# Causal attention with memory and a gated MLP: pairing the mask matmuls, one addition on VectorE, the feature's exponential to SBUF, updates out of the turning step

## The chip, the cores and the metric

The kernel runs on one core of a Trainium2 chip, as one program. The metric is the device time of an execution in microseconds (us). The core's engines work side by side, each through its own queue in order: TensorE (PE; its weight loads are PEld), VectorE (DVE), ScalarE (ACT), GpSimd (POOL) and SyncE (SP), which issues the transfers (DMA). SBUF is the working memory, PSUM the memory that matmuls write.

## The reference, cut to what matters

```python
def _layernorm(x, axis=-1, eps=1e-5): (x - mean) / sqrt(var + eps)

def _A_ref(x, wq, wk, wv, wo, beta):          # attention with memory, S=2048, D=640
    H = 32; Dh = D // H; N = 4; L = S // N    # Dh = 20, L = 512
    q, k, v = x @ wq, x @ wk, x @ wv          # each as (B, H, N, L, Dh)
    phi = lambda t: where(t > 0, t + 1.0, exp(t))
    M = 0; z = 0
    for s in range(N):
        logits = einsum("bhqd,bhkd->bhqk", qs, ks) * Dh ** -0.5 + mask   # causal, -1e9
        a_dot = softmax(logits) @ vs
        a_mem = (phi(qs) @ M) / (phi(qs) . z + 1e-6)
        o = g * a_mem + (1.0 - g) * a_dot     # g = sigmoid(beta), per head
        M = M + phi(ks)^T @ vs;  z = z + sum_l phi(ks)
    return o @ wo

def _B_ref(x, w_in, w_sp, b_sp, w_out):       # gated MLP, F = 1728, Fh = 864
    z = gelu(x @ w_in);  z1 = z[..., :Fh];  z2 = layernorm(z[..., Fh:])
    g = w_sp @ z2 + b_sp                      # mixes the 2048 rows
    return (z1 * g) @ w_out

x = x + _A_ref(layernorm(x));  x = x + _B_ref(layernorm(x))   # twice, same weights
```

## The kernel before

Every float32 operand of a large matmul is split into a high and a low float16 part, and a product is three matmuls (high by high, high by low, low by high). Each of the two layers has three stages: attention (class `Attention`, L594), the MLP's input half with the last four row tiles of attention's output (`phase1b`, L302), and the spatial half (`phase2`, L400). The change touches attention alone.

**The loop of attention.** `run` (L1034) goes through 64 pairs of heads (4 segments of 512 rows, 16 pairs each). Five steps `t` deal with two pairs; `STEPS` (L533) says what a step takes. In a step, in this order:

- `combine` (L1002) finishes an earlier pair: VectorE scales `pv` (PSUM) into `ab` (SBUF, four row tiles by two heads by 41 columns, of which `a` is the product with v's high part and the row sum, `b` that with v's low part), then GpSimd adds: in the first segment `o = a + b` (L1018); in later ones, where `o` already holds the memory's part, `a = a + o` (L1017) and then L1018.
- `by_queries` (L936) makes logits with queries on the partitions (`mp`, one PSUM buffer), and VectorE takes the maxima of the rows (L959; L956 for two heads' tiles at once) into `mxs`.
- `by_keys` (L905) makes them with keys on the partitions (`es`, one PSUM buffer), and ScalarE takes the exponential into P (L933). Only the causal part is made: key tile j has 512 - 128 j columns of queries. `POFF` (L530) is where a tile lies in P's 1280 columns, `KCH` and `QCH` say which tiles share a step.
- `maxes` (L973), in the turning step (every fifth, t % 5 = 2): the maxima are turned by TensorE (`mtp`, in the one small PSUM buffer "ms"), split into two parts `mr` by ScalarE and VectorE (L981), and written by DMA into rows of the queries, so that `es` comes out with the maximum subtracted.
- work that was posted for this step: `out` (below) and its like.
- `pvs` (L986): TensorE multiplies P's high and low parts PH and PL by v. `cast` (L962) makes PH on ScalarE and PL on GpSimd (in two halves of 640 columns).
- `until` spreads dense projections over the steps: `value` (v, `vps`), `unit` (q and k, `qps`, `kps`) and `project` (output, `yps`). They share two PSUM buffers "dn", so a third has to wait until one of them is read out. `read` (L806, `num`) reads the memory and `update` (L839, `mup`) adds to it, both in the buffer "ms".

**The mask.** After the logits of a step, `emit` (L889) adds -60000 x 60000 or 0 to each diagonal tile by two matmuls for each of two heads (`mask`, L880): a step matrix as weights, a 64-column identity `g.eye` as what moves, 64 columns each. Where a step has two tiles, it has two diagonal tiles, so eight such matmuls.

**The features.** `out` (L763) reads a finished q or k projection: its high part (ScalarE, L770), relu (L773), low part (VectorE, L774). In the same step, later in the program, `features` (L782) takes the exponential in place in PSUM (L783) and VectorE makes min(exp, 1) + relu (L786 for q, L788 for k). Segment 0 needs no q features, segment 3 no k features: 30 of each in the two layers. For k, `keys` (L791) splits the result again (L793, L794), a DMA turns it into `pk` (one buffer), and `update` is posted at least three steps later in a step whose t % 5 is in `UPD` (L537) and which is not that of a read or the one behind it.

**What sets the order.** TensorE's order is the program's own (`manual_schedule`, L1199). On the other engines a scheduler orders the instructions by a model of their times, with the restriction that later work of a step stays behind its maximum or exponential (`behind`).

## Time and profile before

| | |
|---|---|
| median of 3 runs | 2308.2 us (2304.68 to 2310.23) |
| the profiled execution | 2313.21 us, its span 2311.5 us |
| granted TensorE clock, mean | 0.986 |
| first attention | about 75 to 600 us |
| second attention | about 1190 to 1735 us |
| TensorE, busy slices of 40 | 5 to 9 tenths, mostly 8 and 9 |

A profile is of one execution. The span runs from the first to the last instruction on the core, and the device time lies 1.7 us over it. In a group's row stand line, engine, operation, what it writes and reads, its shape, its count, then the busy time, the mean of one in ns, and the idle time before it with who ended it. "Who waited" rows give us and times. TensorE's matmuls are pipelined: the busy time counts the whole of each, though the next begins before it ends.

### The profile page before, as it was taken

What the parts mean: (1) busy time and instruction counts of PE and PEld (TensorE: products, weight loads), DVE (VectorE), ACT (ScalarE), POOL (GpSimd) and SP (SyncE); (2) the same over time, 40 slices, a digit from 0 to 9 for tenths busy, and PEclk for the clock granted to TensorE, in tenths of its full rate; (3) what the DMA queues carried; (4) which work ended last, traced back from release to release, by engine and by line L of the source; (5) the groups of instructions that cost most, each with busy time, mean ns of one, the idle gap of its engine ahead of it and who ended that gap; (6) DMA issues with size and microseconds to landing.
All of it is one profiled execution on the core that took longest, in us unless ns stands there. A gap on an engine that the chain in (4) does not pass through costs nothing.

```text
span 2311.5 us, 52604 instructions
## 1 busy us (share of the span) xinstructions
PE 2167.8 (94%) x21706; PEld 1306.2 (57%) x21706; DVE 1372.8 (59%) x2577; ACT 1139.0 (49%) x1344; POOL 987.0 (43%) x976
## 2 busy tenths in 40 slices
PE   5888889999899999999998989999989999999998
PEld 3455555666555555555554556566665555555554
DVE  7678878777754544343327786777756443534331
ACT  3578788888532322121126987888863322212110
POOL 2387889999610000000104988899991100000000
PEclk9999999999899999999999999999999999999999
DMA  5566665345743687566634465443565347756561
GB/s 167 148 159 157 169 165 133 84 119 133 212 127 86 150 231 158 160 156 162 148 86 107 113 149 144 124 102 106 139 172 127 94 118 201 164 155 163 154 147 47
DMA packets 512113, 325.60 MB, mean 141 GB/s; under 512 B 411488, under 2 KB 454368, under 8 KB 507520
## 3 DMA queue, kind: packets, MB, share of 16 engines
q1 hardware_dynamic: 511872, 322.23, 54.5%
q8 instruction: 170, 2.79, 0.5%
q14 instruction: 71, 0.58, 0.1%
HBM read 148.46 MB, written 85.61 MB: 101 GB/s over the span
## 4 chain that ended last, share of the span: by engine, by line
PE 56%; DMA 4%; POOL 4%; DVE 3%; ACT 3%; issue 2%; SPq 1%; DVEq 0%; ACTq 0%; POOLq 0%
PE gp L450 23%; PE zp L363 13%; PE cyp L479 8%; POOL PL L970 3%; PE qps L756 2%; PE pv L998 2%; PE vps L697 2%; PE kps L756 1%; PE mp L895 1%; DMA th<-xnhl 1%; PE yps L729 1%; PE yp L340 1%; ACT P L933 1%; PE es L895 1%; DVE mxs L959 1%
## 5 line engine op out<-in xcount | busy, mean ns | idle before, releaser
L970 POOL TENSOR_TENSOR PL<-P,PH 128x640 f16<-128x640 f32 x380 | 535.5, 1434 | 53.3 <-PE pv L998 43.6
L450 PE MATMUL gp<-zh,wt 128*128 128x432 f16 x2048 | 462.3, 346 | 0.0
L450 PEld LDWEIGHTS <-wt 128*128 128x128 f16 x3072 | 300.5, 98 | 257.6
L959 DVE TENSOR_REDUCE mxs<-mp 128x2 f32<-128x1024 f32 (+2 forms) x384 | 320.0, 861 | 140.5 <-PE mp L886 139.0
L933 ACT ACTIVATE P<-es,sc 128x1024 f32<-128x1024 f32 (+1 forms) x256 | 271.5, 1060 | 99.1 <-PE es L886 84.9
L465 POOL MEMSET un<- 128x64 f16 x32 | 5.0, 155 | 665.9 <-DMA ut<-un 632.7
L363 PEld LDWEIGHTS <-th 128*128 128x128 f16 x1920 | 188.6, 99 | 173.5 <-DMA th<-xnhl 9.7
L450 PE MATMUL gp<-zl,wt 128*128 128x432 f16 x1024 | 270.6, 346 | 0.0
L453 ACT ACTIVATE u<-gp,bsp,un 128x864 f32<-128x864 f32 x32 | 34.2, 1070 | 431.1 <-PE gp L450 419.6
L968 ACT CAST PH<-P 128x1280 f16<-128x1280 f32 x192 | 239.7, 1248 | 1.6
L272 POOL TENSOR_TENSOR lnrs<-lnve,mhalf 128x1 f32<-128x1 f32 x96 | 60.2, 635 | 421.2 <-DVE lnve L271 374.5
L427 DVE TENSOR_REDUCE am<-wr 128x1 f32<-128x2048 f32 x32 | 73.1, 2286 | 210.2 <-DMA wr<-in_B_w_sp_dram 210.2
L970 POOL TENSOR_TENSOR PL<-Pb,PH 128x640 f16<-128x640 f32 x124 | 177.1, 1454 | 12.4 <-PE pv L998 8.0
L697 PE MATMUL vps<-wvh,xt 128*128 128x320 f16 x640 | 156.6, 313 | 25.5 <-DVE relu L788 19.6
L479 PE MATMUL cyp<-wuh,ut 128*128 128x320 f16 (+1 forms) x896 | 165.1, 301 | 5.8 <-DMA ut<-un 5.8
L895 PEld LDWEIGHTS <-qk 64*128 64x128 f16 (+1 forms) x2048 | 78.2, 94 | 160.4 <-issue 140.0
L479 PEld LDWEIGHTS <-ut 128*128 128x128 f16 (+1 forms) x1344 | 132.1, 98 | 61.6 <-DMA ut<-un 6.6
L998 PE MATMUL pv<-vs,PL 128*128 128x41 f16 x2560 | 157.0, 181 | 4.7 <-POOL PL L970 4.3
L998 PE MATMUL pv<-vs,PH 128*128 128x41 f16 x2560 | 159.5, 182 | 1.1 <-DVE ab L1014 0.8
L363 PE MATMUL zp<-wi1h,th 128*128 128x432 f16 x640 | 151.2, 352 | 7.8 <-DMA th<-xnhl 7.6
L895 PE MATMUL es<-qk 64*128 64x512 f16 (+3 forms) x1024 | 124.8, 300 | 27.7 <-ACT P L933 20.1
L363 PE MATMUL zp<-wi0h,th 128*128 128x432 f16 x640 | 148.3, 346 | 0.0
(189 smaller groups left out, 4294.5 us busy)
## 6 DMA issues: line engine op xcount, KB each, us to landing
wr<-in_B_w_sp_dram SPq DMA_DIRECT2D x32, 1024.0 KB
qk<-st SPq DMA_DIRECT2D x256, 120.0 KB
z<-z SPq DMA_DIRECT2D x32, 432.0 KB
cz<-z SPq DMA_DIRECT2D x32, 432.0 KB
xt<-in_A_x_dram SPq DMA_DIRECT2D x32, 320.0 KB
st<-qhl SPq DMA_DIRECT2D x40, 256.0 KB
st<-khl SPq DMA_DIRECT2D x40, 256.0 KB
x<-x SPq DMA_DIRECT2D x32, 320.0 KB
```

Of the source, the lines that this page charges most:

```text
L363: nc.tensor.matmul(zp[:, n, :FHH], a[:, k, :], b[:, k, c:c + FHH], start=(k == 0 and j == 0), stop=(k == KD - 1 and j == 2))
L427: nc.vector.tensor_reduce(am, wr, AX.X, ALU.max, apply_absolute_value=True)
L450: nc.tensor.matmul(gp[:, n, :FHH], wt[:, k // 8, a, k % 8, :], b[:, k, n * FHH:(n + 1) * FHH], start=(k == 0 and j == 0), stop=(k == NT - ...
L479: nc.tensor.matmul(yp[:, n, :320], a[:kn[k], k, :], b[:kn[k], k, n * 320:(n + 1) * 320], start=(k == 0 and j == 0), stop=(k == KO - 1 and ...
L697: nc.tensor.matmul(ps, a[:, k, c], b[:, k, n * 320:(n + 1) * 320], start=(i == 0), stop=(i == 14))
L756: nc.tensor.matmul(ps, a[:, k, c], b[:, k, :], start=(i == 0), stop=(i == 14))
L895: nc.tensor.matmul(out[:, h, o:o + w], a[r, ac], b[r, bc], start=o == 0, stop=False, skip_group_check=True)
L933: g.exp = nc.scalar.activation(P, E, AF.Exp, scale=g.esc)
L959: e = nc.vector.tensor_reduce(mx[:, :, n, j], mp[:, :, o:o + w], AX.X, ALU.max)
L968: nc.scalar.copy(PH, P[:, h])
L970: (nc.gpsimd if h == 0 or n < self.N - self.TAIL else nc.vector).tensor_tensor(PL[:, c], P[:, h, c], PH[:, c], ALU.subtract)
L998: nc.tensor.matmul(pv[:, i, h, :], x[:, c:c + 128], v[:, j, h0 + h, :], start=(j == 0 and x is PH), stop=(j == i and x is PL), skip_group_ ...
```

## The change

Four edits:

- **Mask.** Where a step has two tiles, one matmul adds the mask to both diagonal tiles: the identity is there twice (128 columns) and the output is a view of two pieces of 64 columns. For that the second key step takes tiles 3 and 1 in this order, and P's columns change places (`POFF`).
- **Additions.** The first addition of `combine` goes from GpSimd to VectorE, and is now `a + b`; the one with the memory's part stays on GpSimd. In the first segment none is left on GpSimd.
- **Features.** The exponential is taken right behind relu, and into a tile `fe` in SBUF (one buffer) rather than in place in PSUM.
- **Updates.** `pk` gets a second buffer, and `UPD` loses the 2, the turning step.

```diff
--- before.py
+++ after.py
@@ -527,14 +527,14 @@
 NU = 5
 UH = [range(6 * m, 6 * m + 6) if m < 4 else range(24, 32) for m in range(NU)]
 TH = [range(min(128 * m // DH, UH[m][0]), (128 * m + 127) // DH + 1) for m in range(NU)]
-POFF = [0, 512, 1024, 896]
-KCH = ((0,), (1, 3), (2,))
+POFF = [0, 640, 1024, 512]
+KCH = ((0,), (3, 1), (2,))
 QCH = ((3,), (2, 0), (1,))
 STEPS = ((0, 0, 0), (0, 1, 0), (0, 2, 1), (1, 0, 0), (1, 1, 0))
 BIG = 60000.0
 PVS = ((0, 5, 0), (0, 6, 1), (1, 8, 0), (1, 8, 1))
 CAST = ((0, 2, 0), (0, 3, 1), (1, 4, 0), (1, 5, 1))
-UPD = (2, 3, 4, 0)
+UPD = (3, 4, 0)
 RD = (-6, -1, 9, 14, 24)
 
 
@@ -543,16 +543,17 @@
 
 
 
-    g.eye = cp.tile([128, 64], F16, name="eye")
+    g.eye = cp.tile([128, 128], F16, name="eye")
     g.step = {nm: cp.tile([128, 192], F16, name="step" + nm) for nm in "qk"}
     with tc.tile_pool(name="tmp", bufs=1) as tp, tc.tile_pool(name="acp", bufs=1, space=PSUM) as pp:
         f = tp.tile([128, 192], F32, name="fmask")
-        for t, n, b, sg, op in ((g.eye, 64, 0, 1, ALU.not_equal), (g.step["q"], 192, -64, 1, ALU.is_ge), (g.step["k"], 192, 64, -1, ALU.is_ge)):
+        for t, n, b, sg, op in ((g.eye[:, :64], 64, 0, 1, ALU.not_equal), (g.step["q"], 192, -64, 1, ALU.is_ge), (g.step["k"], 192, 64, -1, ALU.is_ge)):
             nc.vector.memset(f, 0.0)
             for h in range(2):
                 v = f[64 * h:64 * h + 64, :n]
                 nc.gpsimd.affine_select(v, v, [[sg, n]], op, BIG if op is ALU.not_equal else -BIG, base=b, channel_multiplier=-sg)
             nc.vector.tensor_copy(t, f[:, :n])
+        nc.vector.tensor_copy(g.eye[:, 64:], g.eye[:, :64])
 
         g.gate = cp.tile([128, H], F32, name="gate")
         g.iomg = cp.tile([128, H], F32, name="iomg")
@@ -771,31 +772,31 @@
             if feature:
                 r = self.u2.tile([128, L], F32, tag="tmp", name="relu")
                 nc.scalar.activation(r, ps, AF.Relu, scale=g.rq if q else g.rk)
+                e = self.u1.tile([128, L], F32, tag="fe", name="fe")
+                nc.scalar.activation(e, ps, AF.Exp, scale=g.rq if q else g.rk)
             nc.vector.scalar_tensor_tensor(hl[:, 1], ps, QS, hl[:, 0], ALU.mult, ALU.subtract)
             self.stack(nm, s, m, hl)
             if feature:
                 if self.now is None:
-                    features(r)
+                    features(r, e)
                 else:
-                    self.half.setdefault(self.now, []).append(lambda: features(r))
-
-        def features(r):
-            nc.scalar.activation(ps, ps, AF.Exp, scale=g.rq if q else g.rk)
+                    self.half.setdefault(self.now, []).append(lambda: features(r, e))
+
+        def features(r, e):
             if q:
                 self.phq[m] = self.u4.tile([128, L], F32, tag="phq", name="phq")
-                nc.vector.scalar_tensor_tensor(self.phq[m], ps, 1.0, r, ALU.min, ALU.add)
+                nc.vector.scalar_tensor_tensor(self.phq[m], e, 1.0, r, ALU.min, ALU.add)
             else:
-                nc.vector.scalar_tensor_tensor(r, ps, 1.0, r, ALU.min, ALU.add)
+                nc.vector.scalar_tensor_tensor(r, e, 1.0, r, ALU.min, ALU.add)
                 self.post(3 if self.now is not None and self.now < -5 else 1, lambda: keys(r))
 
         def keys(ph):
             hl = self.u2.tile([128, 2, L], F16, tag="hl", name="phl")
             nc.scalar.mul(hl[:, 0], ph, g.sig)
             nc.vector.scalar_tensor_tensor(hl[:, 1], ph, g.sig, hl[:, 0], ALU.mult, ALU.subtract)
-            self.pk_of = s, m
-            self.pk = self.u1.tile([128, 2, 4, 128], F16, tag="pk", name="pk")
-            nc.sync.dma_start(self.pk.rearrange("p i t c -> p (i t) c"), hl.rearrange("p i c -> p (i c)"), transpose=True)
-            work = lambda: self.update(s, m)
+            pk = self.u2.tile([128, 2, 4, 128], F16, tag="pk", name="pk")
+            nc.sync.dma_start(pk.rearrange("p i t c -> p (i t) c"), hl.rearrange("p i c -> p (i c)"), transpose=True)
+            work = lambda: self.update(s, m, pk)
             if self.now is None:
                 self.half.setdefault(-8, []).append(work)
             else:
@@ -836,11 +837,10 @@
 
         self.post(1, out)
 
-    def update(self, s, m):
+    def update(self, s, m, pk):
 
         g, nc = self.g, self.nc
-        assert self.pk_of == (s, m), (self.pk_of, s, m)
-        pkh, pkl = self.pk[:, 0], self.pk[:, 1]
+        pkh, pkl = pk[:, 0], pk[:, 1]
         n = len(TH[m])
         hs = slice(TH[m][0], TH[m][0] + n)
         v = self.vs[s % 2]
@@ -881,10 +881,15 @@
 
         g, nc = self.g, self.nc
         r = slice(64 * h, 64 * h + 64)
-
-        c = o + 64 * s
-        nc.tensor.matmul(out[:, c:c + 64], g.step[nm][r, 64 - 64 * s:192 - 64 * s], g.eye[r], start=False, stop=s == 1,
-                         skip_group_check=True)
+        n = len(o)
+        if n == 1:
+            v = out[:, h, o[0] + 64 * s:o[0] + 64 * s + 64]
+        else:
+            d = o[1] - o[0]
+            b = o[0] - o[0] % d
+            v = out[:, h, b:b + 2 * d].rearrange("p (n r c) -> p n r c", n=2, c=64)[:, :, (o[0] - b) // 64 + s, :]
+        e = g.eye[r, :64] if n == 1 else g.eye[r].rearrange("p (n c) -> p n c", n=2)
+        nc.tensor.matmul(v, g.step[nm][r, 64 - 64 * s:192 - 64 * s], e, start=False, stop=s == 1, skip_group_check=True)
 
     def emit(self, todo):
 
@@ -893,10 +898,10 @@
             for h in range(2):
                 r = slice(64 * h, 64 * h + nr)
                 nc.tensor.matmul(out[:, h, o:o + w], a[r, ac], b[r, bc], start=o == 0, stop=False, skip_group_check=True)
+        out, nm, o = todo[0][0], todo[0][8], [e[9] for e in todo]
         for half in range(2):
-            for out, _, _, _, _, _, _, _, nm, o in todo:
-                for h in range(2):
-                    self.mask(out[:, h], nm, h, o, half)
+            for h in range(2):
+                self.mask(out, nm, h, o, half)
 
     def pair(self, n):
 
@@ -1013,9 +1018,9 @@
         ab = self.pl2.tile([128, 4, 2, 41], F32, tag="ab", name="ab")
         nc.vector.tensor_tensor(ab, T, rs.unsqueeze(3).to_broadcast((128, 4, 2, 41)), ALU.mult)
         a, b = ab[:, :, :, 0:DH], ab[:, :, :, DH + 1:]
+        nc.vector.tensor_tensor(a if s > 0 else o, a, b, ALU.add)
         if s > 0:
-            nc.gpsimd.tensor_tensor(a, a, o, ALU.add)
-        nc.gpsimd.tensor_tensor(o, a, b, ALU.add)
+            nc.gpsimd.tensor_tensor(o, a, o, ALU.add)
         if h0 + 2 < UH[m][-1] + 1:
             return
 
```

**ScalarE, a k projection of the first segment.** `khl`, `relu` and `kps` (now `fe`) are the projection's high part, relu and exponential, `phl` the high part of the feature, P the exponentials of the logits, PH their high part, `mr` the turned maxima. Before:

```order
L770 ACTIVATE khl<-kps 128x512
L773 ACTIVATE relu<-kps,sc 128x512
L933 ACTIVATE P<-es,sc 128x2x512
L783 ACTIVATE kps<-kps,sc 128x512
L933 ACTIVATE P<-es,sc 128x2x256
L933 ACTIVATE Pb<-es,sc 128x2x256
L979 ACTIVATE mr<-mtp 16x128
L702 ACTIVATE vs_283<-vps 128x16x20
L968 CAST PH<-P 128x1280
L793 ACTIVATE phl<-relu,sc 128x512
```

and now:

```order
L771 ACTIVATE khl<-kps 128x512
L774 ACTIVATE relu<-kps,sc 128x512
L776 ACTIVATE fe<-kps,sc 128x512
L938 ACTIVATE P<-es,sc 128x2x512
L795 ACTIVATE phl<-relu,sc 128x512
L938 ACTIVATE P<-es,sc 128x2x256
L938 ACTIVATE Pb<-es,sc 128x2x256
L984 ACTIVATE mr<-mtp 16x128
L703 ACTIVATE vs_284<-vps 128x16x20
L973 CAST PH<-P 128x1280
```

The exponential moved from behind a P to ahead of it, and the feature's high part `phl` up by several places.

**VectorE, a k projection's low part and what follows it.** `wap` is background work on weights, `mxs` are maxima, `relu<-` the product of the feature, `gm<-ab` the new addition; the brackets name the queues whose signal an instruction waits for (DMAHW are transfers, Activation is ScalarE). Before:

```order
L774 SCALAR_TENSOR_TENSOR khl<-kps,khl 128x512 [waits DMAHW4_49,Activation_49]
L1010 RECIPROCAL rs<-rs 128x8 [waits DVE_49]
L1014 TENSOR_TENSOR ab<-pv,rs 128x328 [waits DVE_49,Pool_49]
L959 TENSOR_REDUCE mxs_289<-mp 128x2 [waits PE_49]
L248 TENSOR_REDUCE wap<-wmst 128x1 [waits DMAHW3_49]
L788 SCALAR_TENSOR_TENSOR relu<-kps,relu 128x512 [waits Activation_49]
L981 SCALAR_TENSOR_TENSOR mr<-mtp,mr 16x128 [waits DMAHW1_49,DMAHW7_49,DMAHW0_49,Activation_49]
L794 SCALAR_TENSOR_TENSOR phl<-relu,sc,phl 128x512 [waits DMAHW5_49,Activation_49]
L959 TENSOR_REDUCE mxs_289<-mp 128x2 [waits PE_49]
```

and now:

```order
L777 SCALAR_TENSOR_TENSOR khl<-kps,khl 128x512 [waits DMAHW5_49,Activation_49]
L790 SCALAR_TENSOR_TENSOR relu<-fe,relu 128x512
L1019 TENSOR_TENSOR ab<-pv,rs 128x328 [waits DVE_49]
L964 TENSOR_REDUCE mxs_290<-mp 128x2 [waits PE_49]
L248 TENSOR_REDUCE wap<-wmst 128x1 [waits DMAHW3_49]
L1021 TENSOR_TENSOR gm<-ab 128x4x40 [waits DVE_49]
L796 SCALAR_TENSOR_TENSOR phl<-relu,sc,phl 128x512 [waits DMAHW6_49,DMAHW5_49,Activation_49]
L986 SCALAR_TENSOR_TENSOR mr<-mtp,mr 16x128 [waits DMAHW4_49,DMAHW1_49,Activation_49]
L964 TENSOR_REDUCE mxs_290<-mp 128x2 [waits PE_49]
```

The product moved up to directly behind `khl` and has no wait of its own; the addition is new, and `ab` no longer waits for GpSimd.

**TensorE, a turning step of the first segment.** `mtp` is the turning of the maxima, `qps` a projection, `mup` an update, `mp` the next step's query product. Before:

```order
L886 MATMUL es<-eye,stepk 128x64
L977 MATMUL mtp<-ident,mxs_289 16x128
L756 LDWEIGHTS wqh
L756 MATMUL qps<-xt_286,wqh 128x512
L756 LDWEIGHTS wql
L756 MATMUL qps<-xt_286,wql 128x512
L849 LDWEIGHTS pk
L849 MATMUL mup<-vs_282,pk 128x168
```

and now:

```order
L892 MATMUL es<-eye,stepk 128x2x64
L982 MATMUL mtp<-ident,mxs_290 16x128
L757 LDWEIGHTS wqh
L757 MATMUL qps<-xt_287,wqh 128x512
L757 LDWEIGHTS wql
L757 MATMUL qps<-xt_287,wql 128x512
L900 LDWEIGHTS qk_278
L900 MATMUL mp<-qk_278 128x384
```

The mask's matmul has two pieces of 64 columns, and the update is gone from this step: it stands in the step behind it, among the next projection's matmuls. In each layer five of 15 updates moved so, by one step.

## Prediction

> **What bounds the kernel now.** I read the page's first part, then the busy time by stretches, then the chain of waits, then who waited for whom.
>
> ```profile
> PE 2167.8 (94%) x21706; PEld 1306.2 (57%) x21706; DVE 1372.8 (59%) x2577; ACT 1139.0 (49%) x1344; POOL 987.0 (43%) x976
> PE 56%; DMA 4%; POOL 4%; DVE 3%; ACT 3%; issue 2%; SPq 1%; DVEq 0%; ACTq 0%; POOLq 0%
> ```
>
> TensorE is the bound of the whole, but the change touches only the two attention stages (about 75 to 600 us and 1190 to 1735 us). The chain of the second row adds up to about 73% of the span: it is followed back only to about 628 us, so its POOL, DVE and ACT shares come from the second attention almost alone. The stretches split each attention into two unlike halves (columns: us, then busy us of PE, PEld, DVE, ACT, POOL, the granted clock, DMA share, GB/s):
>
> ```profile
> 115.00:395.00 280.00, 241.79 (x3584) 150.63 (x3584) 227.99 (x418) 225.94 (x285) 231.91 (x206) 0.96 0.61 157
> 395.00:555.00 160.00, 154.85 (x2529) 103.36 (x2528) 118.24 (x222) 134.94 (x157) 154.70 (x146) 1.00 0.42 108
> 1230.00:1510.00 280.00, 256.82 (x3897) 160.78 (x3899) 216.39 (x395) 234.81 (x291) 237.60 (x213) 0.99 0.50 125
> 1510.00:1670.00 160.00, 154.82 (x2525) 103.36 (x2523) 118.83 (x223) 135.53 (x160) 154.72 (x147) 1.00 0.42 113
> ```
>
> In the first half no engine is full: PE 86% and 92%, DVE 81% and 77%, POOL 83% and 85%. In the second half PE and POOL both stand at 97% and DVE falls to 74%. The chain of the second attention, asked for each half, says the same:
>
> ```profile
> by line: PE qps L756 9.9%; PE pv L998 7.9%; issue 7.4%; PE kps L756 7.3%; PE mp L895 6.8%; DVE mxs L959 4.9%; ACT P L933 4.7%; PE es L895 4.3%; PE vps L697 4.1%; DVE phl L794 3.9%; ACT PH L968 3.4%; PE yps L729 2.3%; DVE mxs L956 2.2%; PE m
> by line: POOL PL L970 26.1%; issue 8.0%; PE yps L729 7.0%; PE pv L998 6.8%; PE mp L895 4.2%; PE vps L697 3.3%; PE qps L756 3.3%; ACT PH L968 3.2%; PE es L895 3.1%; ACT P L933 3.1%; POOL ohl L1027 3.0%; DMA th<-xnhl 3.0%; POOL gm L1018 2.9%;
> ```
>
> The first row is 1230 to 1510 us: PE's own work, and DVE with at least 4.9 + 3.9 + 2.2 = 11%. The second is 1510 to 1735 us: POOL leads. So an edit that relieves POOL is worth something in the second half, and one that loads DVE costs something in the first.
>
> **Features out of PSUM.** A projection's PSUM buffer (two of them, for v, q, k and output) was free only after the feature's VectorE step L788 or L786; now after the low part `khl`/`qhl` and the exponential. Who waited for L788:
>
> ```profile
>   PE vps L697: 19.6, 9
>   PE kps L756: 4.4, 5
>   PE yps L729: 1.3, 3
> ```
>
> That is 25.3 us in which TensorE stood still. How much earlier is the buffer free? One of the waits in order of time:
>
> ```profile
> 304.32 0.69 ACT L773 ACTIVATE relu<-kps,sc 128x512 f32<-128x512 f32 x1
> 305.05 0.69 DVE L774 SCALAR_TENSOR_TENSOR khl<-kps,khl 128x512 f16<-128x512 f32 x1 [0.54 <-ACT relu L773]
> 306.44 0.68 ACT L783 ACTIVATE kps<-kps,sc 128x512 f32<-128x512 f32 x1
> 307.73 0.68 DVE L788 SCALAR_TENSOR_TENSOR relu<-kps,relu 128x512 f32<-128x512 f32 x1
> 308.46 0.30 PE L729 MATMUL yps<-woh,o 128*128 128x320 f16 x1 [0.64 <-DVE relu L788]
> ```
>
> In the rows of the new order the product `relu<-fe` waits for no engine, so the wait of `khl` ahead of it covers ScalarE's exponential too: relu's end at 305.01, plus 0.68 for the exponential, plus 0.69 for `khl`, is 306.38, against 308.41 before: 2.0 us earlier, more than the wait of 0.64. At the start of an attention, where the four steps follow each other without a gap, less is gained:
>
> ```profile
> 1213.54 0.70 DVE khl L774
> 1214.26 0.67 ACT kps L783
> 1214.96 0.70 DVE relu L788
> 1215.70 1.38 PE vps L697 x9
> ```
>
> Here `khl` would end at 1213.54 + 0.67 + 0.70 = 1214.91 instead of 1215.66 for the product: 0.8 us of gain, where TensorE had waited 2.8. Taking two such waits as mostly staying, about 20 of the 25.3 us are cut. What is late next is VectorE's own backlog (it made the product late), which TensorE meets again at the next maximum. I keep two thirds, **-13 us**; bounds 0 and -25.
>
> ScalarE's sum does not change; its exponential stands one place earlier, ahead of a P that waits 0.68 us longer, where it used to delay a later P as much: 0.
>
> **Update one step later.** Waits for the mask row's low part `mr` (of the shared small buffer), and those a read has behind an update:
>
> ```profile
>   DVE mr L981: 8.4, 8
>   PE num L821: 4.9, 6
> ```
>
> The 8.4 us go. In TensorE's order three more updates in each layer now stand one step ahead of a read, and such a neighbour cost 4.9 / 6 = 0.8 us: +4.9. Net -3.5, of which two thirds: **-2 us**; bounds -8 and +1. The second `pk` buffer lets the transposing DMA on SP's queue start without waiting for the update before it; what is queued behind it on SP is fetches issued steps ahead, so I count 0.
>
> **One mask matmul for two tiles.**
>
> ```profile
> L886 PE MATMUL es<-eye,stepk 64*128 64x64 f16 x2048 | 84.2, 191 | 0.0
> L895 PE MATMUL es<-qk 64*128 64x128 f16 x256 | 28.7, 217 | 0.0
> L895 PE MATMUL es<-qk 64*128 64x256 f16 x256 | 25.0, 271 | 8.4 <-ACT P L933 8.4
> ```
>
> 1536 of the 4096 mask matmuls go, but those left carry 128 columns instead of 64. From 128 to 256 columns costs 54 ns, so 64 more cost 27 (217 - 191 says 26), the width of the one that goes: **0**. The busy column (84.2 us / 2048 = 41 ns each) would make it 63 us of TensorE time; it counts latencies that overlap. I keep 0 and -12 as bounds (a fifth of the 63, were some of it issue time). The tiles' new places in P change only which half of PL the second row of pv products needs; PL's two halves follow one another on POOL as before: 0.
>
> **The additions.** POOL loses one addition in each of 128 pairs:
>
> ```profile
> L1018 POOL TENSOR_TENSOR gm<-ab x128: 457/471/1380, 111.7 to 1733.0; 128x160 f32<-128x160 f32 x128
> L1017 POOL TENSOR_TENSOR ab<-ab,gm x96: 486/500/1089, 255.5 to 1732.4; 128x160 f32<-128x160 f32 x96
> ```
>
> That is 128 x 0.49 = 62 us of POOL work, worth its price only where POOL is on the path: L1018 has 2.9% of the 225 us of the second half, 6.5 us, and L1017 stands beside it at about the same; one of the two goes: -6.5 in each layer, **-13 us**. VectorE takes 128 additions. Nothing like them stands in the trace of before; the nearest in size is L855 (0.32 us each), which reads one input from PSUM. The additions read both from SBUF, and so now do the 60 features. The only such step in the loop is the low part of the keys:
>
> ```profile
> L855 DVE TENSOR_TENSOR mst<-mup,bmask x30: 293/320/323, 78.7 to 1534.8; 128x168 f32<-128x168 f32 x18, 128x147 f32<-128x147 f32 x12
> L788 DVE SCALAR_TENSOR_TENSOR relu<-kps,relu x30: 668/681/692, 58.5 to 1516.7; 128x512 f32<-128x512 f32 x30
> L794 DVE SCALAR_TENSOR_TENSOR phl<-relu,sc,phl x30: 741/1172/1957, 59.9 to 1518.8; 128x512 f16<-128x512 f32 x30
> L794 DVE SCALAR_TENSOR_TENSOR phl<-relu,sc,phl 128x512 f16<-128x512 f32 x30 | 37.1, 1236 | 7.7 <-ACT phl L793 7.7
> ```
>
> With a PSUM input (L788) the spread is 24 ns; with two SBUF inputs (L794) the same width takes 741 to 1957. One of them, and POOL at that time:
>
> ```profile
> 365.12 1.86 DVE L794 SCALAR_TENSOR_TENSOR phl<-relu,sc,phl 128x512 f16<-128x512 f32 x1
> 365.03 3.21 POOL L970 TENSOR_TENSOR PL<-P,PH 128x640 f16<-128x640 f32 x2
> L970 POOL TENSOR_TENSOR PL<-P,PH x380: 1387/1400/2000, 99.7 to 1719.9; 128x640 f16<-128x640 f32 x190
> ```
>
> VectorE began just after a PL subtraction, and took as long as that one's 1.40 us plus some 0.5; the pair of PL took 3.21 instead of 2.80. So each holds the other up: VectorE by 1236 - 741 = 0.49 us on average, POOL by up to 0.41.
>
> The Trainium skill (SBUF — State Buffer, "Who interferes with whom") says that VectorE with two SBUF inputs and a GpSimd instruction that reads SBUF exclude each other for a whole instruction, while one SBUF input contends with nothing. By that rule the old place in PSUM was the free one and the change gives it up; the trace agrees (24 ns of spread against 1216), and the sum by the rule is the one that follows.
>
> VectorE's added time: 128 x (0.32 + 0.49) = 104 us, and 60 x (0.06 + 0.49) = 33 us. Half of the additions and 49 of the 60 features fall in the first halves:
>
> ```profile
> 0.00:395.00 395.00, 15.72 (x24) 0.96 0.60 157
> 1190.00:1510.00 320.00, 17.04 (x25) 0.99 0.49 124
> ```
>
> (stretches of L783's exponentials). So 52 + 27 = 79 us there, 58 in the second halves. The price is the share of VectorE on the path: in the first half between the 11% of the chain's row and the page's 3% of 2311.5 us, 69 us, over some 300 us, 23%; I take a fifth: **+16 us** (bounds 0 and +79). The instruction behind each addition is a maximum, and behind the maximum waits TensorE's next query product, with one PSUM buffer. In the second half VectorE has a quarter of its time free: **+2**. POOL's hold-ups there, 11 features by 0.41 and 64 additions by 0.05 (most of an addition's 0.32 is start-up outside the hold, as 0.33 of L794's 0.74 is), are 8 us on an engine with a third of the chain: **+3**.
>
> **Sum:** -13 - 2 + 0 - 13 + 16 + 2 + 3 = -7 us against the profiled execution, whose device time is 2313.2 us (span 2311.5): 2306. The runs shown have a median of 2308.2, so about **2301 us**.
>
> **The rivals.**
> - *VectorE becomes the bound of the first half.* It decides when VectorE's busy time reaches about 97% of the stretch, where POOL sets the pace in the second half. 228 + 40 of 280 us is 96% in the first layer, 216 + 40 is 91% in the second. Then half of the 79 us is on the path, +40; features keep a quarter, -5; update 0; POOL -13; the rest +5: +27, **2335 us** at the full price, about 2322 if only the first layer does it. For it: the new order puts 101 of the 128 additions straight before a maximum. Against it, VectorE before stood still 139 us for query products, and an addition that falls into such a wait costs nothing:
>
> ```profile
> L959 DVE TENSOR_REDUCE mxs<-mp 128x2 f32<-128x1024 f32 (+2 forms) x384 | 320.0, 861 | 140.5 <-PE mp L886 139.0
> ```
>
> - *The gains are taken back:* TensorE, freed from the features, waits as long at the maxima. Features -4, update 0, POOL -13, costs +18: **2309 us**, no change.
> - *The waits all turn into time:* features -20, update -3.5, POOL -20 (its whole subtraction queue moves up in the second half), VectorE +10: **2275 us**. For it: TensorE's idle time in both attentions is what the change aims at; against it: nothing else is idle beside it.
> - *The masks cost per instruction:* the -12 above on top of the forecast: **2289 us**. The columns speak against it.
>
> **How the numbers follow.** Forecast (2292 to 2303): 0.36. VectorE bound (2313 to 2335): 0.28. Taken back (2304 to 2312): 0.20. All waits (2270 to 2288): 0.11. Masks by count: 0.05. A change of 0.2%, 4.6 us, is about what can be told from none. Faster 0.36 + 0.11 + 0.05 = 0.52, same 0.20, slower 0.28. The range 2274 to 2324 leaves out the far ends of the two outer cases, about 2 in 10.
>
> **What would show it.** Right: no wait of vps, kps or yps for a feature, none of mup for `mr`; `phq<-fe` and `relu<-fe` at some 1.2 us instead of 0.68; additions at 0.4 to 1 us with a wide spread; POOL below 95% in the second half and that half shorter. Wrong: more waiting of the query products for the maxima, or VectorE over 95% of the first half (the first rival); a second half of unchanged length with POOL less busy (then TensorE bounds it); mask rows whose total falls with their count.

## The result, and the profile after

The changed kernel takes 2325.7 us (median of 4 runs, 2322.6 to 2329.7) against 2308.2 us (2304.7 to 2310.2) for the kernel before, measured beside it: a ratio of 1.0073, 95% interval [1.0058, 1.0088]. It is slower by 17 us; the forecast was 2301, and the range ended at 2324. The profiled execution has a span of 2323.9 us, 12.4 more than the one of before.

The page's first part and the first row of its chain:

```profile
PE 2170.0 (93%) x20170; PEld 1300.1 (56%) x20170; DVE 1476.3 (64%) x2706; ACT 1139.7 (49%) x1344; POOL 951.0 (41%) x848
PE 32%; DVE 7%; ACT 2%; issue 2%; DMA 2%; POOL 1%; SPq 0%; DVEq 0%; ACTq 0%; POOLq 0%
```

VectorE's busy time grew by 103.5 us, GpSimd's fell by 36. TensorE's is the same within 2.2 us. The four stretches of before, of the changed kernel (us, busy us of PE, PEld, DVE, ACT, POOL, clock, DMA share, GB/s):

```profile
115.00:395.00 280.00, 240.55 (x3163) 147.17 (x3163) 249.19 (x441) 222.21 (x278) 219.90 (x171) 0.94 0.57 151
395.00:555.00 160.00, 148.47 (x2108) 97.67 (x2110) 134.01 (x233) 127.09 (x150) 140.00 (x118) 0.98 0.40 108
1230.00:1510.00 280.00, 257.79 (x3464) 159.00 (x3465) 234.79 (x421) 229.59 (x285) 225.30 (x176) 0.99 0.49 124
1510.00:1670.00 160.00, 146.40 (x2007) 93.47 (x2006) 133.13 (x230) 124.97 (x150) 137.19 (x115) 0.95 0.38 105
```

The surprise is in the second and fourth row. In the second halves GpSimd fell from 97% to 88 and 86% of the stretch, VectorE rose from 74% to 84 and 83%, far from full, and TensorE fell from 97% to 93 and 92%: the half got longer though the engine at the head of its chain was relieved. The granted clock fell as well, from 1.00 to 0.98 and 0.95; it is taken up below. Four of the things that TensorE waits for (the view of waits, whole run; us, times, longest):

```profile
PE mp L900 <- DVE mxs L964: 29.0, 37, 4.0
PE mp L900 <- DVE mxs L961: 13.4, 15, 2.4
PE num L822 <- DVE mst L855: 7.9, 10, 1.5
PE vps L698 <- DVE khl L777: 5.6, 3, 2.7
```

The query products `mp` waited 8.9 + 2.8 = 11.7 us for the maxima before, now 42.4. The waits of `vps`, `kps` and `yps` for a feature (25.3 us) and of `mup` for `mr` (8.4 us) are gone; what is left of the former is about 7 us for `khl` and `qhl`. The groups by line:

```profile
L961 DVE TENSOR_REDUCE mxs<-mp 128x4 f32<-128x1024 f32 x64 | 77.8, 1216 | 9.1 <-PE mp L892 9.0
L1021 DVE TENSOR_TENSOR ab<-ab 128x160 f32<-128x160 f32 x96 | 79.2, 825 | 2.6
L1021 DVE TENSOR_TENSOR gm<-ab 128x160 f32<-128x160 f32 x32 | 20.8, 652 | 0.9
L790 DVE SCALAR_TENSOR_TENSOR relu<-fe,relu 128x512 f32<-128x512 f32 x30 | 29.8, 994 | 0.0
L788 DVE SCALAR_TENSOR_TENSOR phq<-fe,relu 128x512 f32<-128x512 f32 x30 | 28.1, 937 | 0.0
L892 PE MATMUL es<-eye,stepk 64*128 64x128 f16 x768 | 54.3, 218 | 0.0
L892 PE MATMUL es<-eye,stepk 64*128 64x64 f16 x512 | 29.7, 191 | 0.0
```

The additions take 79.2 + 20.8 = 100.0 us, as worked out (104). The features' products are near 0.97 us rather than 1.2. The key masks' busy time is 54.3 + 29.7 = 84.0 us, against 84.2 before. The first row, beside its fellow of before, shows the trouble:

```profile
L956 DVE TENSOR_REDUCE mxs<-mp 128x4 f32<-128x1024 f32 x64 | 78.3, 1223 | 30.8 <-PE mp L886 30.5
```

VectorE used to arrive early at 43 of these 64 maxima and wait 30.5 us in all for the product; now it does so at 14 of them, for 9.0 us, so it mostly arrives late, and TensorE waits for it.

**A measure by pairs.** In each trace the 128 instructions `rs<-pv` (the first of `combine`) mark the pairs. For the table I took their starts, counted from pair 0 of the layer, and subtracted the same of before; both layers are added. "Outside" is the rest of the span. It is one profiled execution for each kernel, and that may lie some us from the median beside it: the one of before took 2313.2 us, 5.0 over its median, the changed kernel's lies at its median. Part of the excess can be placed. From the first `zp` product to the last `gp` product, almost wholly in stages whose code is the same, both layers of before take 1118.1 us and those of the changed kernel 1110.8, and before's second layer is there the longest of all 17 profiles. So 7.3 us of the -11.3 outside lie where the change edits nothing, and the columns inside the attentions say more than the outside and the span. Pairs 40 to 56 are a steady stretch: TensorE, VectorE and GpSimd are busy there to 0.02 us alike in both layers of the kernel before.

| kernel | pairs 0-40 | 40-56 | 56-63 | outside | span | median, us (before) | ratio, 95% |
|---|---|---|---|---|---|---|---|
| changed | +19.4 | +9.4 | -5.1 | -11.3 | +12.4 | 2325.7 (2308.2) | 1.0073 [1.0058, 1.0088] |
| e1_add | +7.6 | +9.8 | -1.8 | -1.8 | +13.8 | 2325.1 (2307.7) | 1.0077 [1.0064, 1.0089] |
| e2_feat | +11.2 | +5.6 | -0.9 | -6.3 | +9.6 | 2316.3 (2307.7) | 1.0031 [1.0021, 1.0041] |
| e3_upd | -0.2 | 0.0 | -2.6 | -2.8 | -5.6 | 2305.6 (2307.7) | 0.9995 [0.9986, 1.0004] |
| e4_mask | -4.0 | -0.2 | +0.1 | +2.8 | -1.2 | 2313.1 (2307.7) | 1.0020 [1.0009, 1.0030] |
| e5_noadd | +5.4 | +2.5 | -1.3 | -9.2 | -2.6 | 2309.7 (2306.9) | 1.0009 [0.9995, 1.0022] |
| e6_two_sbuf | +13.5 | +8.4 | -3.3 | +18.1 | +36.6 | 2348.8 (2306.9) | 1.0178 [1.0158, 1.0199] |
| e7_one_psum | +8.4 | +0.7 | +0.5 | +6.2 | +15.8 | 2331.6 (2306.9) | 1.0103 [1.0084, 1.0121] |
| e8_add_late | +9.8 | -0.8 | -4.8 | -1.0 | +3.3 | 2316.0 (2306.9) | 1.0036 [1.0023, 1.0049] |
| e9_feat_late | -0.8 | +6.1 | -0.4 | -9.1 | -4.2 | 2309.7 (2310.4) | 1.0001 [0.9989, 1.0013] |
| e10_add_psum | +30.2 | -0.8 | +4.9 | -6.7 | +27.6 | 2340.6 (2310.4) | 1.0135 [1.0115, 1.0155] |
| e11_after_late | +11.7 | +0.8 | -4.5 | -10.3 | -2.3 | 2309.9 (2310.4) | 0.9996 [0.9984, 1.0007] |
| e12_late_half | -0.4 | -0.8 | -3.7 | -3.7 | -8.6 | 2308.4 (2310.4) | 0.9994 [0.9981, 1.0007] |
| e13_combined | +4.1 | -0.8 | -3.2 | -10.8 | -10.7 | 2302.6 (2308.1) | 0.9980 [0.9964, 0.9996] |
| e14_after_feat_late | +12.2 | +12.1 | -5.8 | -12.7 | +5.8 | 2326.6 (2308.1) | 1.0075 [1.0061, 1.0090] |
| e15_after_both_late | +5.5 | +2.1 | -3.1 | -5.6 | -1.1 | 2304.6 (2308.1) | 0.9983 [0.9972, 0.9994] |

Kernels that share a median of before were measured together with it on one chip (the first row apart).

**Idle time and clock.** In pairs 0 to 40 TensorE loses time in two ways. The rows of both layers, of before and then of the changed kernel:

```profile
109.10:454.40 345.30, 303.62 (x4590) 193.28 (x4585) 276.19 (x510) 280.03 (x350) 294.66 (x265) 0.97 0.57 146
1253.50:1574.40 320.90, 296.59 (x4595) 190.18 (x4594) 245.29 (x455) 271.18 (x336) 290.31 (x265) 0.99 0.49 122
105.80:460.80 355.00, 309.57 (x4110) 194.02 (x4106) 309.59 (x550) 281.03 (x350) 285.06 (x225) 0.94 0.54 143
1258.70:1589.30 330.60, 301.81 (x4116) 190.66 (x4115) 276.07 (x496) 270.89 (x336) 282.49 (x225) 0.97 0.46 118
```

It stands still for 74.2 us there (length less busy time) where it was 66.0: 8.2 of the 19.4 us. The other part falls to a lower granted clock: length times what the clock lacks is about 14 us before and 31 in the changed kernel, an upper bound on what it costs. The traces have the clock at half in pieces of 3.4 us or a multiple, and each such piece from 85 us on to 30 us from the end, in all 17 profiles, begins behind 3.4 us in which TensorE was busy for at most 65%. So a pause of TensorE is followed by slower matmuls; no run varies the clock by itself. In the steady stretch it explains little: the clock is full there in the changed kernel's first layer (+4.5 us) and in e1's second (+4.2), as in before.

### The profile page after: what moved, and what is told of

The parts are those of the page before. It is cut to its first block, busy times and chain, and to the rows that moved or that the text cites. A ratio compares the mean times of both kernels' runs of the same rounds, so it can differ in the third digit from the quotient of the medians.

```text
span 2323.9 us, 49575 instructions
## 1 busy us (share of the span) xinstructions
PE 2170.0 (93%) x20170; PEld 1300.1 (56%) x20170; DVE 1476.3 (64%) x2706; ACT 1139.7 (49%) x1344; POOL 951.0 (41%) x848
## 5 line engine op out<-in xcount | busy, mean ns | idle before, releaser
L975 POOL TENSOR_TENSOR PL<-P,PH 128x640 f16<-128x640 f32 x380 | 545.4, 1463 | 85.6 <-PE pv L1003 59.3
L900 PEld LDWEIGHTS <-qk 64*128 64x128 f16 (+1 forms) x2048 | 83.9, 94 | 190.2 <-issue 171.6
L900 PE MATMUL mp<-qk 60*128 60x512 f16 (+3 forms) x1024 | 127.5, 306 | 45.9 <-DVE mxs L964 29.0
```

What stands on the lines that cost most here:

```text
L900: nc.tensor.matmul(out[:, h, o:o + w], a[r, ac], b[r, bc], start=o == 0, stop=False, skip_group_check=True)
L975: (nc.gpsimd if h == 0 or n < self.N - self.TAIL else nc.vector).tensor_tensor(PL[:, c], P[:, h, c], PH[:, c], ALU.subtract)
```

## The experiments

### Each part alone, and all but the additions

**e1_add**, the additions' edit alone on the kernel before:

```diff
-        if s > 0:
-            nc.gpsimd.tensor_tensor(a, a, o, ALU.add)
-        nc.gpsimd.tensor_tensor(o, a, b, ALU.add)
+        nc.vector.tensor_tensor(a if s > 0 else o, a, b, ALU.add)
+        if s > 0:
+            nc.gpsimd.tensor_tensor(o, a, o, ALU.add)
```

> The kernel before with the additions' edit alone. Theory 1 (VectorE's additions are the loss: they have two SBUF inputs, wait for GpSimd's instruction, and hold up the maxima behind them): +12 to +20 us against before, VectorE about 100 us busier, GpSimd about 60 us less busy, more waiting of the query products for the maxima. Theory 2 (the features' new place is the loss): -4 to +4 us. Theory 3 (the mask's new form or P's new order is the loss): -4 to +4 us.

**e2_feat**, the features' edit alone (exponential behind relu, to SBUF):

```diff
                 nc.scalar.activation(r, ps, AF.Relu, scale=g.rq if q else g.rk)
+                e = self.u1.tile([128, L], F32, tag="fe", name="fe")
+                nc.scalar.activation(e, ps, AF.Exp, scale=g.rq if q else g.rk)
...
-            nc.scalar.activation(ps, ps, AF.Exp, scale=g.rq if q else g.rk)
...
-                nc.vector.scalar_tensor_tensor(r, ps, 1.0, r, ALU.min, ALU.add)
+                nc.vector.scalar_tensor_tensor(r, e, 1.0, r, ALU.min, ALU.add)
```

> The kernel before with the features' edit alone. Theory 1: -10 to 0 us: TensorE's 25 us of waits for the features go, VectorE gains some 17 us of busy time. Theory 2 (ScalarE's exponential, now ahead of a P, and VectorE's product with two SBUF inputs are the loss): +8 to +18 us. Theory 3: -10 to 0 us.

**e3_upd**, the update's edit alone (`UPD` without the 2, `pk` with two buffers):

```diff
-UPD = (2, 3, 4, 0)
+UPD = (3, 4, 0)
...
-            self.pk = self.u1.tile([128, 2, 4, 128], F16, tag="pk", name="pk")
+            pk = self.u2.tile([128, 2, 4, 128], F16, tag="pk", name="pk")
```

> The kernel before with the second pk buffer and the updates out of the turning step alone. All theories: -5 to +2 us; the 8.4 us of waits of mup for mr go, and some 4 us of waits of reads for an update come.

**e4_mask**, the mask's edit alone (its hunks of the diff, in `POFF`, `KCH`, `eye`, `mask` and `emit`):

```diff
-POFF = [0, 512, 1024, 896]
-KCH = ((0,), (1, 3), (2,))
+POFF = [0, 640, 1024, 512]
+KCH = ((0,), (3, 1), (2,))
```

> The kernel before with the mask's edit alone (tiles 3 and 1 in this order, P's columns changed). Theories 1 and 2: -3 to +3 us, since the columns streamed are the same. Theory 3: +8 to +18 us, from waits of pv for the second half of PL or slower matmuls with an output in two pieces. If the mask cost went by the number of matmuls: -8 to -12 us.

**e5_noadd**, the changed kernel with its additions back on GpSimd (e1's diff backwards):

> The changed kernel with both additions back on GpSimd as before (mask, features and updates stay). If the edits add up: +8 (features) + 5 (mask) - 2 (update) = +11 us against before. If the additions are all of the changed kernel's loss and the others only look bad alone: -3 to +3 us.

Measured, as differences of the medians: additions +17.5 us (theory 1), features +8.6 (theory 2), update -2.1 (within the measurement, as all theories had it), mask +5.4 (between the theories), and the last three together +2.8, which cannot be told from none (e5's second reading). The additions alone lose what the changed kernel loses. The parts do not add up: features, update and mask come to 12 us one by one and to 2.8 together. The additions' mark in the groups of e1 is the one seen in the changed kernel:

```profile
L1016 DVE TENSOR_TENSOR ab<-ab 128x160 f32<-128x160 f32 x96 | 81.1, 845 | 2.5
L956 DVE TENSOR_REDUCE mxs<-mp 128x4 f32<-128x1024 f32 x64 | 77.8, 1216 | 7.5 <-PE mp L886 7.4
```

The mask is odd: its pairs got 4 us shorter and its profiled execution 1.2, while its median rose by 5.4. Its profile adds its time outside the pairs, in stages without a mask (+5.2 us between the last pair of the first attention and the first of the second). Against before's profile, which lies 5.0 us over its median, a profile 1.2 us shorter fits a higher median (e4's lies 1.1 under its own); why those stages took longer the trace does not say, and it stays open.

### What in an addition costs: time, hold or place

**e6_two_sbuf** and **e7_one_psum** leave the kernel before as it is and add one addition to each pair, at the place of e1's, whose result nobody reads: in e6 with both inputs in SBUF, in e7 with one of them in PSUM. Each has one of the last two lines.

```diff
+        x = self.pl2.tile([128, 4, 2, DH], F32, tag="xtra", name="xtra")
+        nc.vector.tensor_tensor(x, a, b, ALU.add)                      # e6
+        nc.vector.tensor_tensor(x, T[:, :, :, 0:DH], b, ALU.add)       # e7
```

> The kernel before with one more VectorE addition in each pair, of the same size, at the same place and with the same two SBUF inputs (a + b of the same tile), whose result nobody reads; GpSimd keeps both of its own. Theory 1a (the loss is that such an addition and GpSimd's instruction exclude each other): +15 to +28 us, more than the additions' edit, since GpSimd is not relieved and is held up as well. Theory 1b (the loss is any VectorE work ahead of the maxima): +8 to +20 us, and the same as in the run with one PSUM input.

> As the run with two SBUF inputs, but the extra addition takes its first input from pv in PSUM (the unscaled a) and its second from ab in SBUF; the result is read by nobody, and the pair's PSUM buffer is held some 0.3 us longer. Theory 1a: +0 to +8 us, each such addition at 0.3 us without spread. Theory 1b: +8 to +20 us, as much as with two SBUF inputs.

**e8_add_late** is e1 with the additions posted behind the maximum of the step (the added lines):

```diff
+        def first():
+            nc.vector.tensor_tensor(a if s > 0 else o, a, b, ALU.add)
+            if s > 0:
+                nc.gpsimd.tensor_tensor(o, a, o, ALU.add)
+
+        self.half.setdefault(self.now, []).append(first)
```

> The additions' edit alone, with both additions posted behind the step's maximum instead of ahead of it. Theory 1a: +8 to +16 us, a little under the +17.5 us of the edit, since the waits for GpSimd stay as long. Theory 1b: -5 to +5 us, since the maximum that TensorE waits for is no longer behind an addition.

Measured: +41.9, +24.7 and +9.1 us. e6 and e7 cost more than either reading allowed. Part of that is no matter of additions: the MLP's first steps follow the attention's last pairs in another way. In the first layer 31 products `pv` still come behind the first `zp` in before, in e6 and e7 none, and `zp` begins 5.4 us ahead of the last pair's mark in before, 9.2 and 5.2 us behind it in e6 and e7. The outside column holds 18.1 and 6.2 us. In e6 TensorE's wait there is plain:

```profile
PE zp L363 <- DMA th<-xnhl: 19.4, 4, 10.4
```

That was 7.6 us before. So the whole times of e6 and e7 mislead, and the steady stretch has to be read alone. There the answer is clean: with two SBUF inputs +8.4 us in 32 pairs, with one PSUM input +0.7, and with two SBUF inputs but behind the maximum (e8) -0.8. The stretch of 440 to 550 us, in before, e1, e7 and e8 (columns as above):

```profile
440.00:550.00 110.00, 107.34 (x1747) 69.91 (x1747) 81.71 (x151) 93.85 (x108) 105.64 (x101) 1.00 0.40 113
```

```profile
440.00:550.00 110.00, 103.20 (x1643) 66.23 (x1642) 89.55 (x160) 89.94 (x104) 95.38 (x80) 0.98 0.37 105
```

```profile
440.00:550.00 110.00, 107.50 (x1743) 69.38 (x1742) 85.07 (x168) 94.01 (x109) 105.31 (x100) 1.00 0.38 108
```

```profile
440.00:550.00 110.00, 107.68 (x1752) 68.94 (x1750) 90.83 (x165) 93.81 (x109) 100.12 (x85) 1.00 0.38 106
```

TensorE is busy 107.3 of 110 us before, 103.2 with the additions ahead of the maximum, and 107.5 and 107.7 in the two others. e8's VectorE is as busy as e1's (90.8 against 89.6 us) and TensorE loses nothing: place, not load. And GpSimd is 5.5 us less busy in e8 than before, yet pairs 40 to 56 are only 0.4 us shorter in each layer. By its time e8 falls under theory 1a, but not for its reason: where the hold had cost time, nothing is left of the loss, and the 9.1 us lie elsewhere (e12).

**e10_add_psum** asks the same of the real addition: the product in two halves, one left in PSUM, so that the addition at e1's place has one PSUM input.

```diff
-        nc.vector.tensor_tensor(ab, T, rs.unsqueeze(3).to_broadcast((128, 4, 2, 41)), ALU.mult)
-        a, b = ab[:, :, :, 0:DH], ab[:, :, :, DH + 1:]
+        a, b = T[:, :, :, 0:DH], ab[:, :, :, DH + 1:]
+        r = rs.unsqueeze(3).to_broadcast((128, 4, 2, DH))
+        nc.vector.tensor_tensor(b, T[:, :, :, DH + 1:], r, ALU.mult)
+        nc.vector.tensor_tensor(a, a, r, ALU.mult)
+        x = ab[:, :, :, 0:DH] if s > 0 else o
+        nc.vector.tensor_tensor(x, a, b, ALU.add)
         if s > 0:
-            nc.gpsimd.tensor_tensor(a, a, o, ALU.add)
-        nc.gpsimd.tensor_tensor(o, a, b, ALU.add)
+            nc.gpsimd.tensor_tensor(o, x, o, ALU.add)
```

> The additions' part alone, with the first addition on VectorE at the same place ahead of the maximum, but as product of each half apart (one left in PSUM) and an addition with one PSUM input: no VectorE instruction of it has two SBUF inputs. VectorE's added time is then about 0.5 us a pair without spread, against 0.8 with the hold. Theory A (in the second half it is the hold ahead of the maximum that costs, in the first half any VectorE time): first half (pairs 0 to 32 of both layers) about 8 us more than before, pairs 32 to 56 within 2 us of before, time 2312 to 2318. Theory B (the added work costs the same however it is done): 2322 to 2328, with 7 to 10 us more in pairs 32 to 56. Against both: the next step's value products wait longer for the PSUM bank, since the addition reads it too (up to 0.5 us a pair, some 10 us).

Measured: +30.2 us, slower than both theories had it, but with the loss at the other end: pairs 40 to 56 take 0.8 us less than before, pairs 0 to 40 take 30.2 more, 23.4 of it in the first layer. One line of it (duration in ns as min/median/max, then who waited):

```profile
L1019 DVE TENSOR_TENSOR ab<-pv,ab x96: 302/324/326, 277.2 to 1766.2; 128x160 f32<-128x160 f32 x96
...
  POOL gm L1021: 28.9, 18
  PE pv L998: 16.7, 10
```

The hold is gone (24 ns of spread), and with it the loss of the steady stretch. Now the value products wait 16.7 us for the PSUM bank that the addition still reads. In the first layer's pairs 0 to 40 TensorE stands still 13.6 us longer and its clock is 0.94 against 0.97; the two together cover the 23.4 us there, though the clock's part is not measured by itself.

The traces show the hold one by one. In the changed kernel 105 of the 128 additions begin while a GpSimd instruction runs. 87 take over 0.4 us, and all of these end 0.18 us behind that GpSimd instruction's end; the 23 that begin beside none take at most 325 ns. In e10 100 begin beside one, and none takes over 326 ns.

**e12_late_half** is e8 for the last two segments (pairs 32 to 63) only (the added lines; `first` adds into `a`):

```diff
+        if s >= 2:
+            self.half.setdefault(self.now, []).append(first)
+        else:
+            if s > 0:
+                nc.gpsimd.tensor_tensor(a, a, o, ALU.add)
+            nc.gpsimd.tensor_tensor(o, a, b, ALU.add)
```

> The additions on VectorE behind the step's maximum, only in the last two of the four query segments (pairs 32 to 63 of a layer); in the first two they stay on GpSimd as before. Theory A (the loss of 9.1 us with all of them behind the maximum sits in the first half): first half as before, pairs 32 to 63 between 4 us less and 2 us more over both layers: 2303 to 2309. Theory B (VectorE work costs some 0.07 us a pair wherever it is): half the loss, 2311 to 2313.

Measured: -2.0 us, no difference from before, as theory A had it. The 9 us that e8 still lost sit in the first half: 9.8 us in pairs 0 to 40 with all additions moved, -0.4 with none moved there.

### The features

**e9_feat_late** is e2 with the exponential left where the kernel before has it, only into `fe`:

```diff
-        def features(r, e):
+        def features(r):
+            e = self.u1.tile([128, L], F32, tag="fe", name="fe")
+            nc.scalar.activation(e, ps, AF.Exp, scale=g.rq if q else g.rk)
```

> The features' part alone, but with the exponential at the place on ScalarE where the kernel before has it (behind the posted step), only its target moved to SBUF. Theory A (what cost 8.6 us in the part alone is the exponential's earlier place, which holds up the scores' exponentials behind it): the time falls back to the kernel before, 2305 to 2309, and pairs 32 to 56 of each layer take what they took before, within 1 us. Theory B (it is the product with two SBUF inputs, 1.2 us on VectorE against 0.68, ahead of what TensorE waits for): the loss stays, 2313 to 2318, with 3 to 6 us more in pairs 32 to 56 of each layer.

Measured: -0.7 us, no difference, where e2 lost 8.6. So alone it was the earlier place. TensorE's waits in e2, and then in e9:

```profile
PE es L896 <- ACT P L934: 28.7, 31, 2.8
PE mp L896 <- DVE mxs L960: 22.0, 25, 2.0
PE es L896 <- ACT Pb L934: 4.3, 6, 2.0
PE mp L896 <- DVE mxs L957: 2.5, 5, 0.8
```

```profile
PE es L896 <- ACT P L934: 21.9, 32, 2.2
PE mp L896 <- DVE mxs L960: 19.1, 33, 2.0
PE vps L697 <- ACT fe L784: 10.6, 4, 3.5
PE mp L896 <- DVE mxs L957: 4.3, 8, 0.8
PE es L896 <- ACT Pb L934: 3.5, 3, 2.1
```

The maxima cost the same in both, 24.5 and 23.4 us against 11.7 before: that is the products with two SBUF inputs. What differs is the key products' wait for the exponentials of the scores, 33.0 against 25.4 us (26.9 before). Theory A had the time right and its detail wrong: e9's pairs 40 to 56 are 6.1 us longer than before, as theory B said of that stretch. In the table 9.1 us outside the pairs make it even, but 4.0 of them lie between the first `zp` and the last `gp`, where before's profile was long, so what makes up for the stretch stays open in part.

### The places in the changed kernel

**e11_after_late**: the changed kernel, additions as in e8. **e14_after_feat_late**: the changed kernel, exponential as in e9. **e15_after_both_late**: both.

> The changed kernel with its additions on VectorE posted behind the step's maximum. Theory A (parts add up: place is worth what it was worth on the kernel before, 17.5 against 9.1 us): 2315 to 2318, with pairs 32 to 56 about 8 us shorter over both layers than in the changed kernel and the first half as in the changed kernel. Theory B (with the other edits VectorE is full and a later place only delays GpSimd's second addition): 2322 to 2327.

> The changed kernel with features' exponential back at its late place on ScalarE (still to SBUF); additions as changed. Theory A (the exponential's earlier place costs in the changed kernel what it costs alone, about 8 us): 2315 to 2319. Theory B (the additions ahead of the maximum set the time by themselves, whatever ScalarE does): 2323 to 2327. A third outcome under 2312 would mean that the two edits only cost together.

> The changed kernel with both put late: features' exponential at the place of before, the additions on VectorE behind the step's maximum. Theory A (the two losses are separate and add up): 2300 to 2304, faster than before. Theory B (with one of them mended the rest is hidden, as the changed kernel with late additions alone already came to the time of before): 2306 to 2311.

Measured: 2309.9, 2326.6 and 2304.6 us: e11 below both expectations, e14 as theory B had it, e15 between the two. Moving the additions behind the maximum takes the loss of 17 us back but for what can't be told from none, twice the 8 that it was worth on the kernel before (e11's pairs 40 to 56 lose 0.8 us instead of 9.4); moving the exponential alone changes nothing (1.0075 against the changed kernel's 1.0073). In e14 the query products wait longer for the maxima than in the changed kernel, 52.1 us:

```profile
PE mp L900 <- DVE mxs L964: 39.9, 43, 2.2
PE mp L900 <- DVE mxs L961: 12.2, 16, 2.9
```

So in the changed kernel the additions ahead of the maximum set the time at either place of the exponential. With them out of the way the exponential's place may be worth something again: e15 is at 0.9983 and e11 at 0.9996, whose intervals overlap.

### A version that keeps what costs nothing

**e13_combined**: the kernel before with e12, e3 and e9, the last only for segments 0 to 2 (segment 3's features are made in the steady stretch):

```diff
+            e = self.u1.tile([128, L], F32, tag="fe", name="fe") if s < 3 else ps
```

> The kernel before with what cost nothing in the runs so far: additions on VectorE behind the step's maximum for the last two of four segments only; features' exponential at its late place, to SBUF for the first three segments and in PSUM as before for the last; the update's edit. Theory A (these gains are real and add up): 2299 to 2305, ratio under 0.998, with pairs 40 to 56 of each layer as before or up to 0.5 us shorter. Theory B (what is gained in one place is waited for in another): 2305 to 2310, no difference from before.

Measured: 2302.6 us against 2308.1, ratio 0.9980 [0.9964, 0.9996]. Theory A held for the time and the steady stretch (0.4 us shorter in each layer), with its bound on the ratio just met, at the edge of what can be told from none; e15, which still has all four edits, comes to the same.

## Why the prediction was wrong

The forecast was -7 us and the medians moved by +17.5, 24.5 us apart. The run e5, the changed kernel without its additions, splits this. Features, update and mask were to bring -15 and came to +2.8; the additions were to cost 16 - 13 + 2 + 3 = +8 and cost the other 14.7. So 17.8 us of the miss lie with the first three and 6.7 with the additions; with the additions taken first (e1), it is 15.0 and 9.5. By place (the changed row of the table less e5's), the additions cost 14.0 us in pairs 0 to 40, where the forecast had +16, and 6.9 - 3.8 = +3.1 in pairs 40 to 63, where the forecast for the second halves was -8. The prediction's halves meet at pair 32; the table is cut at 40, since the update's edit alone moves some 8 us across pair 32 (e3: -7.9 us in pairs 0 to 32, +7.7 in 32 to 40).

- **The step with the wrong mechanism: "In the second half VectorE has a quarter of its time free: +2".** A share of free time says nothing of where the work is put. The additions stand between the scaling and the next maximum; held by GpSimd's subtraction they take 1.02 us there on average (e1, pairs 40 to 56), the maximum comes late, and TensorE, which has one buffer for query products and 2.4% of slack in that stretch (107.34 of 110 us), waits. In pairs 40 to 56 this cost 9.8 us alone (e1). It goes to zero or below behind the maximum (e8) or without the hold (e10), and a further 0.32 us without a hold at the same place cost 0.7 (e7). The first rival had the right mechanism, but put it in the first half alone and let VectorE's busy time decide it: "It decides when VectorE's busy time reaches about 97% of the stretch". It stood at 81% in e1's steady stretch and at 84% in the changed kernel's second half, and had decided all the same.
- **The second: GpSimd's relief, -13.** It was read from GpSimd's share of the chain of the second half. In e8, e10 and e12 GpSimd is 5 to 7 us less busy in 110 us and the additions do no harm there, yet the 32 pairs take 0.8 us less. TensorE was busy 107.3 of 110 us beside it; two engines at 96 and 98% hid each other, and the chain had named one of them. The prediction listed this case as a sign that it is wrong ("a second half of unchanged length with POOL less busy").
- **The third, and the furthest off in size: features, -13.** The step is that two thirds of the cut waits were to become time. The waits for L788 went, as said (25.3 us to about 7), and the late place of the exponential shows what this is worth: nothing (e9: -0.7 us, by its interval -2.5 to +3.0), since the query products take back 12 us of it and the projections still wait 10.6 us for the exponential. The rival "The gains are taken back" had said so of the maxima. The earlier place was put at 0 ("where it used to delay a later P as much: 0"), and this was wrong too: alone it cost some 8 us more (e2 against e9), though in the changed kernel none (e14). The products' 1.2 us was too long by a quarter.
- **First half, +16: near the 14.0 us that the additions cost in the changed kernel's pairs 0 to 40, but partly by luck.** Alone they cost about half of it: 7.6 us in e1, 9.8 in e8 behind the maximum, and -0.4 where they stay on GpSimd (e12); e7's 8.4 without the hold has another cause beside it, since the value products wait 9.3 us there for the PSUM bank that its addition reads. The sum had no term for the granted clock, which holds part of the loss there. That the place behind the maximum does not help there fits other results of VectorE that come later: in e8 TensorE waits 13.9 us for `mr` against 8.4 before, and 7.9 for `mst` against 4.9. The update's edit takes the wait for `mr` away, which may be why late additions cost nothing in e11; no run tries this alone.
- **Update, -2:** right within the measurement; the neighbours it foresaw are there (`num` waits 7.9 us for `mst`, against 4.9). **Mask, 0:** right for the busy time, and the pairs gained 4 us; the median of the part alone rose by 5.4 for a reason that stays open.
- The durations that were worked out held: 100.0 us of additions for 104. GpSimd's busy time fell by 36 us and not by 62: without the additions it had risen by 18.7 (e5). By the rule of the Trainium skill that the prediction weighed (SBUF — State Buffer, "Who interferes with whom"), one PSUM input is free of the hold and two SBUF inputs are not; the traces agree (302 to 326 ns in e10, up to 1.59 us in the changed kernel, the same 160 elements). The rule was used for the length of the work only, and its cost is decided by what stands behind it.

What stays open: why the parts do not add up (29.4 us one by one, 17.5 together), what the clock alone costs, and what the additions meet in the first half.

## What to carry to other kernels

Before an instruction is put on an engine with time to spare, look at what stands behind it in that engine's order and how many buffers the one who waits for that has; in the changed kernel the same additions cost some 15 us ahead of a maximum with a single-buffered reader, and behind it nothing that can be told. An engine's share of the chain is worth its price only if no other engine is as full in the same stretch: ask the busy time of each engine there before counting a relief. An experiment that adds a dummy instruction also moves the order at the seams of the stages, so compare a steady stretch and not the whole time. Read the granted clock beside each stretch: here a pause of TensorE was followed by matmuls at half clock.

## What the runs showed of the hardware that was not expected

The same VectorE addition of two SBUF inputs got shorter at another place: 845 ns on average ahead of the maximum (e1, 96 of them), 679 ns behind it (e8), its shortest 0.30 us:

```profile
L1017 DVE TENSOR_TENSOR ab<-ab 128x160 f32<-128x160 f32 x96 | 65.2, 679 | 0.2
```

The 0.18 us from the end of the GpSimd instruction to the end of the held addition are the same at both places (e1 and e8). So the length of a held instruction depends on when it meets GpSimd, and a duration taken from one place (the 1236 ns of L794 for the features' 970) is an estimate at another.
